# Later weights' maxima, scales and splits spread over layer 1: an interleaved attention and gMLP kernel

## The chip, the cores and the metric

The kernel runs on one core of a Trainium2 chip. The time is the device time of one execution in microseconds (us). A core has five engines that run at once, each with its own instruction queue: TensorE (PE; its weight loads are listed as PEld), VectorE (DVE), ScalarE (ACT), GpSimd (POOL) and SyncE (SP), which here issues all DMA transfers. Engines wait for each other by semaphores, and each one takes its instructions strictly in order: what waits holds up all that is queued behind it. TensorE multiplies from SBUF into PSUM; its clock can be halved for stretches, and the profile lists the granted clock.

## The reference

```python
def _A_ref(x, wq, wk, wv, wo, beta):          # 2048 x 640, 32 heads of 20, 4 segments of 512
    q, k, v = heads of x @ wq, x @ wk, x @ wv
    for s in range(N):
        logits = jnp.einsum("bhqd,bhkd->bhqk", qs, ks) * scale + mask
        a_dot = jnp.einsum("bhqk,bhkd->bhqd", _softmax(logits), vs)
        pq = phi(qs)
        a_mem = einsum(pq, M) / (einsum(pq, z)[..., None] + 1e-6)
        outs.append(g * a_mem + (1.0 - g) * a_dot)
        M = M + einsum("bhld,bhle->bhde", phi(ks), vs);  z = z + phi(ks).sum(l)
    return o @ wo

def _B_ref(x, w_in, w_sp, b_sp, w_out):
    z = _gelu(x @ w_in)                        # w_in 640 x 1728
    z1, z2 = z[..., :Fh], _layernorm(z[..., Fh:])
    g = w_sp @ z2 + b_sp[:, None]              # w_sp 2048 x 2048
    return (z1 * g) @ w_out                    # w_out 864 x 640

x = x + _A_ref(_layernorm(x), ...);  x = x + _B_ref(_layernorm(x), ...)
x = x + _A_ref(_layernorm(x), ...);  x = x + _B_ref(_layernorm(x), ...)
```

The two layers use the same weights.

## The kernel before

Every large product is made of three fp16 matmuls: each operand is split into a high and a low half (h and l), and h·h, h·l and l·h are summed. A weight therefore goes through a chain once, in layer 1: its absolute **maximum** over the whole matrix is found (tile by tile on VectorE, L192, from tiles named wmst into a table wap); a power of two becomes its **scale** (`pow2_max` and `pow2_spread`: the column of maxima is turned with TensorE, wtp, reduced, put on a diagonal, wdg, and spread to all partitions by a second matmul, wbc); and each tile is loaded again (wst) and **split**: the high half by ScalarE (L84), the low half by VectorE (L85). The split weight is then kept in HBM (`keep`, w_oh and so on), and layer 2 only loads it.

There are seven weights. q, k and v are made in the head of the program. The other four are the subject here: o (the attention's output, 640x640), i0 and i1 (the halves of w_in, each 640x864; i1 makes z2 and i0 makes z1) and u (w_out, 864x640).

Layer 1 runs in this order: head; attention over 64 pairs of heads; the mixer's first half (`phase1b`: norm, w_in, gelu, z2's norm, in tiles of 128 tokens, and the attention's output product for four of them); its second half (`phase2`: w_sp, gate, w_out). Layer 2 is the same with another form of the w_sp product (`phase2s`).

In attention a step t is a third of a pair. Each pair has scores computed twice: mp with queries in rows, of which VectorE takes the row maximum mx (L1304), and es with keys in rows, which ScalarE turns to P by exp (L1297). The maxima go through TensorE's transpose mtp (one for each pair) and ScalarE and VectorE's mr into two rows of the tile qk by DMA, so that es comes out with the maximum taken off. ScalarE casts P to PH, GpSimd takes the difference PL (L1315; VectorE does some in the last four pairs), and pv is the product of PH and PL with the values. Between them run the dense products: vps, qps, kps (values, queries, keys), yps (output).

The order on TensorE is written out by hand (`run`: streams of jobs, each with its step t). On the other engines a scheduler orders the instructions from the order of the program text, priorities (`high_priority`) and its own estimate of when things are ready. The stream `background` in `run` placed the work on the four weights: all 32 maxima at 0.75 steps apart from step -8, the scales at steps 50 to 53, o's splits from step 55, i1's from step 69. The tiles for these loads (tag bg, two buffers) are shared with the o tiles of the output product. i0 was loaded and split at the head of `phase1b`, at high priority but into memory that attention's last work still used, with stage tiles of 864 columns.

In `phase1b`, xn is the normed tile, xnhl its two halves, th their transpose, which enters w_in; zp is the product.

Of the kernel before, what the change touches and what calls it, by code (L numbers as in the profile page):

```python
# [46 lines left out]
WNAMES = ["v", "q", "k", "o", "i0", "i1", "u"]  # L47
# [18 lines left out]
def pow2_spread(g, psum, tag, dg, c0, n):  # L66
# [3 lines left out]
    nc.tensor.matmul(bc[:, :n], g.ones8[:n, :], dg[:n, :n], start=True, stop=True)  # L70
    pw = g.pw[:, c0:c0 + n]
    nc.vector.tensor_copy(pw, bc[:, :n])
# [15 lines left out]
class Weight:  # L88
# [17 lines left out]
    def load(self, stage, width=864, tag="wst", keep=True):  # L106
# [4 lines left out]
        if self.made:  # L111
# [5 lines left out]
            return  # L117
        for k in range(self.nk):
# [23 lines left out]
def attn_weights(g, ctx, wv, wq, wk, wo, w_in, w_out):  # L142
# [6 lines left out]
    g.wi = [Weight(g, "i0", 4, w_in, 0, FH), Weight(g, "i1", 5, w_in, FH, FH)]  # L149
# [4 lines left out]
    g.esc, g.rq, g.rk, g.gq, g.gk, g.sig, g.epsd, g.yw, g.zi, g.pofs = s(0), s(1), s(2), s(3), s(4), s(5), s(6), s(7), (s(8), s(9)), s(10)  # L154
# [24 lines left out]
def other_scales(g, a, pool, psum, tag):  # L179

    nc = g.nc
    last = None
    for i, w in enumerate((g.wo, *g.wi, g.wu)):
        width = D if w.cols == D else w.cols // 2
        j = 0
        for k in range(w.nk):
            n = min(128, w.dram.shape[0] - 128 * k)
            for c in range(0, w.cols, width):
                t = a.bg.tile([128, D], F32, tag="bg", name="wmst")[:n, :width]
                nc.sync.dma_start(t, w.dram[k * 128:k * 128 + n, w.c0 + c:w.c0 + c + width])  # L190
                if last is not None:
                    nc.vector.tensor_reduce(*last, AX.X, ALU.max, apply_absolute_value=True)  # L192
                last = g.wap[:n, i, j:j + 1], t
                yield True
                j += 1
    nc.vector.tensor_reduce(*last, AX.X, ALU.max, apply_absolute_value=True)
    yield 50
# [1407 lines left out]
```

## Time and profile before

| | us |
|---|---|
| median of 3 runs | 2320.95 (2319.37 to 2323.72) |
| profiled execution | 2323.64 |
| its span, first to last instruction | 2321.4 |
| layer 1's attention, mtp of the first pair to that of the last | 99.5 to 624.0 |
| layer 1's mixer, first half | 646.7 to 848.6 |
| layer 2's attention, first mtp to last | 1274.8 to 1764.4 |
| layer 2's mixer, first half | 1787.0 to 1979.5 |

A window row gives the busy time of each engine in a stretch, and the share of full clock that TensorE was granted. A group row gives shape, count, busy time, mean duration of one in ns, the idle time of the engine just before, and what ended it. A wait row says who waited for whom: total, times, longest.

### The profile page before, as it was taken

What the parts mean: (1) busy time and instruction counts of PE and PEld (TensorE: products, weight loads), DVE (VectorE), ACT (ScalarE), POOL (GpSimd) and SP (SyncE); (2) the same over time, 40 slices, a digit from 0 to 9 for tenths busy, and PEclk for the clock granted to TensorE, in tenths of its full rate; (3) what the DMA queues carried; (4) which work ended last, traced back from release to release, by engine and by line L of the source; (5) the groups of instructions that cost most, each with busy time, mean ns of one, the idle gap of its engine ahead of it and who ended that gap; (6) DMA issues with size and microseconds to landing.
All of it is one profiled execution on the core that took longest, in us unless ns stands there. A gap on an engine that the chain in (4) does not pass through costs nothing.

```text
span 2321.4 us, 50384 instructions
## 1 busy us (share of the span) xinstructions
PE 2172.0 (94%) x20490; PEld 1298.3 (56%) x20490; DVE 1498.8 (65%) x2792; ACT 1174.5 (51%) x1452; POOL 971.0 (42%) x726
## 2 busy tenths in 40 slices
PE   4878799899989999999999988999998999999999
PEld 2445465556645555556554555656665555555655
DVE  7678868887744545445434788787776767546545
ACT  3379678788732232122212797887875424322321
POOL 2178688888710000000001688888885323000000
PEclk9999899999999999999999999999999999999999
DMA  5654544644662458778555336453467434877875
GB/s 162 165 140 101 128 113 126 131 137 124 149 178 84 134 161 212 230 194 236 165 139 157 75 92 182 107 123 93 121 168 168 113 93 110 252 208 199 211 215 136
DMA packets 509704, 350.14 MB, mean 151 GB/s; under 512 B 409312, under 2 KB 444768, under 8 KB 504352
## 3 DMA queue, kind: packets, MB, share of 16 engines
q1 hardware_dynamic: 509472, 346.93, 56.7%
q8 instruction: 160, 2.62, 0.5%
q14 instruction: 72, 0.59, 0.1%
HBM read 160.83 MB, written 97.93 MB: 111 GB/s over the span
## 4 chain that ended last, share of the span: by engine, by line
PE 65%; DVE 10%; DMA 7%; ACT 7%; issue 3%; POOL 2%; SPq 1%; ACTq 0%; DVEq 0%; POOLq 0%
PE zp L316 14%; PE gp L683 12%; PE cyp L715 3%; PE yps L1098 3%; PE cyp L518 3%; PE pv L1341 3%; DVE mx L1304 3%; PE ga L469 3%; PE kps L1122 3%; ACT P L1297 3%; PE mp L1288 2%; PE qps L1122 2%; PE gb L469 2%; PE vps L1065 2%; ACT PH L1314 2%
## 5 line engine op out<-in xcount | busy, mean ns | idle before, releaser
L1315 POOL TENSOR_TENSOR PL<-P,PH 128x1280 f16<-128x1280 f32 x248 | 649.7, 2622 | 167.2 <-ACT PH L1314 156.9
L1304 DVE TENSOR_REDUCE mx<-mp 128x2 f32<-128x1024 f32 (+3 forms) x512 | 408.8, 818 | 99.6 <-PE mp L1260 98.0
L1297 ACT ACTIVATE P<-es,sc 128x1024 f32<-128x1024 f32 (+1 forms) x384 | 370.3, 964 | 133.9 <-PE es L1260 131.3
L1314 ACT CAST PH<-P 128x1280 f16<-128x1280 f32 x256 | 320.4, 1253 | 22.0 <-PE pv L1341 14.1
L219 POOL TENSOR_TENSOR lnrs<-lnve,mhalf 128x1 f32<-128x1 f32 x92 | 56.0, 618 | 572.4 <-DVE lnve L218 572.4
L316 PEld LDWEIGHTS <-th 128*128 128x128 f16 x1920 | 188.2, 98 | 174.2 <-issue 13.0
L683 PE MATMUL gp<-zh,wt 128*128 128x432 f16 x1024 | 231.4, 346 | 0.2 <-DMA wt<-wn 0.2
L683 PEld LDWEIGHTS <-wt 128*128 128x128 f16 x1536 | 150.2, 98 | 129.4 <-DMA wt<-wn 0.6
L1288 PEld LDWEIGHTS <-qk 60*128 60x128 f16 (+1 forms) x2048 | 91.5, 94 | 226.0 <-issue 154.8
L469 PEld LDWEIGHTS <-wt 128*128 128x128 f16 x1344 | 131.5, 98 | 112.6
L1288 PE MATMUL mp<-qk 60*128 60x512 f16 (+3 forms) x1024 | 138.3, 307 | 42.1 <-DVE mx L1304 41.1
L1341 PE MATMUL pv<-vs,PH 128*128 128x41 f16 x2560 | 168.7, 183 | 1.7 <-DVE ab L1357 1.7
L1260 PEld LDWEIGHTS <-big 64*128 64x128 f16 x3072 | 141.8, 96 | 50.8 <-issue 4.2
L1341 PE MATMUL pv<-vs,PL 128*128 128x41 f16 x2560 | 164.6, 182 | 4.1 <-POOL PL L1315 3.6
L1288 PE MATMUL es<-qk 64*128 64x512 f16 (+3 forms) x1024 | 135.6, 300 | 34.1 <-ACT P L1297 25.4
L1065 PE MATMUL vps<-wvh,xt 128*128 128x320 f16 x640 | 152.5, 304 | 4.8 <-DVE vs L1071 4.1
L1341 PEld LDWEIGHTS <-PH 128*128 128x128 f16 x2560 | 143.1, 96 | 18.5
L316 PE MATMUL zp<-wi1h,th 128*128 128x432 f16 x640 | 148.2, 346 | 2.0 <-DVE x L1104 1.3
L1341 PEld LDWEIGHTS <-PL 128*128 128x128 f16 x2560 | 143.6, 97 | 7.2 <-POOL PL L1315 4.5
L683 PE MATMUL gp<-zl,wt 128*128 128x432 f16 x512 | 135.3, 346 | 0.0
L1122 PE MATMUL kps<-xt,wkh 128*128 128x512 f16 x380 | 122.6, 390 | 9.3 <-DVE phl L1156 9.2
L696 DVE TENSOR_TENSOR u<-u,cz 128x864 f32<-128x864 f32 x16 | 17.0, 1060 | 160.8 <-ACT u L694 114.6
(257 smaller groups left out, 4383.5 us busy)
## 6 DMA issues: line engine op xcount, KB each, us to landing
wr<-in_B_w_sp_dram SPq DMA_DIRECT2D x32, 1024.0 KB
qk<-st SPq DMA_DIRECT2D x256, 120.0 KB
x<-x SPq DMA_DIRECT2D x56, 320.0 KB
z<-z SPq DMA_DIRECT2D x32, 432.0 KB
cz<-z SPq DMA_DIRECT2D x32, 432.0 KB
turned<-wt SPq DMA_DIRECT2D x24, 512.0 KB
wt<-turned SPq DMA_DIRECT2D x24, 512.0 KB
st<-qhl SPq DMA_DIRECT2D x40, 256.0 KB
```

The lines of the kernel that those rows point to most:

```text
L316: nc.tensor.matmul(zp[:, n, :FHH], a[:, k, :], b[:, k, c:c + FHH], start=(k == 0 and j == 0), stop=(k == KD - 1 and j == 2))
L469: nc.tensor.matmul(o[:, :FHH], wt[:, x, m, :], zb[b][:, y, m, :], start=start and i == j == 0, stop=i == NP - 1 and j == 2, skip_group_che ...
L683: nc.tensor.matmul(gp[:, n, :FHH], ready[t][:, k % 2, a, k // 2, :], b[:, k, n * FHH:(n + 1) * FHH], start=(i == 0 and j == 0), stop=(i == ...
L1065: nc.tensor.matmul(ps, a[:, k, c], b[:, k, n * 320:(n + 1) * 320], start=(i == 0), stop=(i == 14))
L1122: nc.tensor.matmul(ps, a[:, k, c], b[:, k, :], start=(i == 0), stop=(i == 14))
L1260: nc.tensor.matmul(out, g.big[r, 64 - 64 * s:192 - 64 * s], mk, start=False, stop=s == 1, skip_group_check=True)
L1288: nc.tensor.matmul(out[:, h, o:o + w], a[r, ac], b[r, bc], start=o == 0, stop=False, skip_group_check=True)
L1297: self.last_of["ACT"] = nc.scalar.activation(P[:, :, 512 * c:512 * c + ew], es[:, :, :ew], AF.Exp, scale=g.esc).ins
L1304: self.last_of["DVE"] = nc.vector.tensor_reduce(self.mx[m][:, :, i], mp[:, :, o:o + w], AX.X, ALU.max).ins
L1314: nc.scalar.copy(PH, P[:, h])
L1315: (nc.gpsimd if h == 0 or n < self.N - self.TAIL else nc.vector).tensor_tensor(PL, P[:, h], PH, ALU.subtract)
L1341: nc.tensor.matmul(pv[:, i, h, :], x[:, c:c + 128], v[:, j, h0 + h, :], start=(j == 0 and x is PH), stop=(j == i and x is PL), skip_group_ ...
```

## The change

It touches five things.

1. **Maxima.** `other_scales` now takes a list of weights, a first step and a pace. o and i1 (15 tiles) are done from step -8 on, 1.9 steps apart; i0 (10 tiles) from step 121, 3 apart; u (7 tiles) in the mixer's first half, a piece after each of its tiles. The tiles have a pool of their own with three buffers, and a tile's maximum is taken two loads later instead of one.
2. **Scales.** The maxima over partitions no longer go through TensorE: the column is stored to a small HBM tensor (wmax), read back by a DMA that gives all of it to every partition (wmall), and reduced on VectorE. This is done three times: o with i1, i0, u. The scale's arithmetic (`pow2_floor`) is the same.
3. **Splits.** A stream of their own, `weights`: o from step 50 at 1.6 steps, i1 from step 124 at 2.4, with a pool of three buffers; each split is issued after the load of the next tile (ahead=1). i0 goes in tiles of 432 columns at the end of layer 1's attention, with a lower priority than before, behind the instructions that the first mixer tile's loads stand behind.
4. **Memory.** The pools of `phase1b` are laid out so that i0's tiles no longer lie on memory that attention's last pairs use; the norm's output goes into the tile it reads or into the x tile; one stage tile of `phase2` moves to the other side. The weights i0 and i1 are kept from within the mixer's loop.
5. The cast and store of an attention output tile (`out` in `combine`) stand one step later, but for the last pair.

```diff
-WNAMES = ["v", "q", "k", "o", "i0", "i1", "u"]
+WNAMES = ["v", "q", "k", "o", "i1", "i0", "u"]
...
-    def load(self, stage, width=864, tag="wst", keep=True):
+    def load(self, stage, width=864, tag="wst", keep=True, ahead=0):
...
-                st = stage.tile([128, 864 if tag == "wst" else D], F32, tag=tag, name="wst")[:n, :w]
+                st = stage.tile([128, {"wst": FH, "w0": FHH}.get(tag, D)], F32, tag=tag, name="wst")[:n, :w]
                 nc.sync.dma_start(st, self.dram[k * 128:k * 128 + n, self.c0 + c:self.c0 + c + w])
+                todo.append((self.h[:n, k, c:c + w], self.l[:n, k, c:c + w], st, self.c))
                 yield
-                split_scaled(self.g, self.h[:n, k, c:c + w], self.l[:n, k, c:c + w], st, self.c)
-                yield
+                if len(todo) > ahead:
+                    split_scaled(self.g, *todo.pop(0))
+                    yield
...
-def other_scales(g, a, pool, psum, tag):
+def other_scales(g, pool, ws, c0, at, pace):
...
-                t = a.bg.tile([128, D], F32, tag="bg", name="wmst")[:n, :width]
+                t = pool.tile([128, D], F32, tag="wm", name="wmst")[:n, :width]
                 nc.sync.dma_start(t, w.dram[k * 128:k * 128 + n, w.c0 + c:w.c0 + c + width])
-                if last is not None:
-                    nc.vector.tensor_reduce(*last, AX.X, ALU.max, apply_absolute_value=True)
-                last = g.wap[:n, i, j:j + 1], t
-                yield True
+                last.append((g.wap[:n, i, j:j + 1], t))
+                if len(last) > 2:
+                    nc.vector.tensor_reduce(*last.pop(0), AX.X, ALU.max, apply_absolute_value=True)
+                yield at
+                at += pace
...
-    nc.vector.tensor_reduce(g.wam[:, 3:7], g.wap, AX.X, ALU.max)
-    yield 51
-    dg = pow2_max(g, pool, psum, tag, g.wam, 3, 4)
-    yield 53
-    pow2_spread(g, psum, tag, dg, 3, 4)
...
+    nc.vector.tensor_reduce(g.wam[:, c0:c0 + n], g.wap[:, c0 - 3:c0 - 3 + n], AX.X, ALU.max)
+    yield at + 3
+    t = pool.tile([128, D], F32, tag="wm", name="wmall")[:, :128 * n]
+    d = nc.dram_tensor(f"wmax{c0}", (128, n), F32, kind="Internal").ap()
+    nc.sync.dma_start(d, g.wam[:, c0:c0 + n])
+    yield at + 6
+    nc.sync.dma_start(t, d.rearrange("(o p) n -> o (p n)", o=1).to_broadcast((128, 128 * n)))
+    yield at + 11
+    nc.vector.tensor_reduce(g.pw[:, c0:c0 + n], t.rearrange("q (p n) -> q n p", n=n), AX.X, ALU.max)
+    pow2_floor(g, c0, n)
...
-        with tc.high_priority(offset=HP if w0 is None else 2 * HP):
-            for _ in g.wi[0].load(sp):
-                pass
...
-            xn = pe1.tile([128, D], F32, tag="xn", name="xn")
+            xn = x1 if t < NWO else xt
...
+        with tc.high_priority(offset=2 * HP) if w0 is not None else first():
+            for _ in g.wi[0].load(sp, FHH, "w0", False, 1):
+                pass
+        more = () if g.wu.made else other_scales(g, wm, (g.wu,), 6, 0, 0)
...
+            if w0 is None and i in (3, 6):
+                g.wi[i == 3].keep()
+            if i > 2:
+                next(iter(more), None)
...
-        self.post(2, out)
+        self.post(2 if n + 1 == self.N else 3, out)
...
+                yield from other_scales(g, self.wm, (g.wo, g.wi[1]), 3, -8, 1.9)
...
+                yield 120
+                yield from other_scales(g, self.wm, (g.wi[0],), 5, 121, 3)
...
+        def weights():
...
+            yield 49
+            for w, width, at, pace in (g.wo, D, 50, 1.6), (g.wi[1], FHH, 124, 2.4):
+                w.tiles(g.top[w is not g.wo])
+                for i, _ in enumerate(w.load(self.ws, width, "ws", w is g.wo, 1)):
+                    yield at + pace * i
```

What stands where on the engines can be read from the two programs. TensorE's order is the same but for two instructions that go, wtp and wbc of the four scales.

On VectorE, around the scales (rs and ab belong to the pair's output, qhl, qps, kps and phl to queries and keys), stood before:

```order
L1357 TENSOR_TENSOR ab<-pv,rs 128x328
L1325 SCALAR_TENSOR_TENSOR mr<-mtp,mr 8x128
L60 TENSOR_REDUCE wmx<-wtp 4x1
L62 TENSOR_SCALAR wdg<-ident,wmx 4x4
L1139 SCALAR_TENSOR_TENSOR qhl<-qps,qhl 128x512
L1144 TENSOR_SCALAR qps<-qps,sc 128x512
L1304 TENSOR_REDUCE mx<-mp 128x2 x2
```

and now, for o and i1, between pairs 11 and 12 instead of 18 and 19:

```order
L1382 TENSOR_TENSOR ab<-pv,rs 128x328
L1329 TENSOR_REDUCE mx<-mp 128x2 x2
L222 TENSOR_REDUCE pw<-wmall 128x2
L1350 SCALAR_TENSOR_TENSOR mr<-mtp,mr 8x128
L1181 SCALAR_TENSOR_TENSOR phl<-kps,sc,phl 128x512
L79 TENSOR_SCALAR pw<-pw 128x2
L1329 TENSOR_REDUCE mx<-mp 128x2
```

The round through TensorE has become one reduction of the tile that came back by DMA.

On ScalarE, at the end of layer 1's attention and the first mixer tiles (z, zh, xnhl), stood before:

```order
L1314 CAST PH<-P 128x1280 x2
L1368 CAST ohl<-oat 128x640
L84 ACTIVATE wi0h<-wst,iv 128x864 x2
L322 ACT_TABLE_LOAD
L322 ACTIVATE z_11256<-zp_11225,sc 128x864
L84 ACTIVATE wi0h<-wst,iv 128x864 x2
L355 CAST zh<-z_11256 128x864
L231 CAST xnhl<-xn 128x640
L84 ACTIVATE wi0h<-wst,iv 128x864
L329 ACTIVATE z_11308<-zp_11277,sc 128x864
```

and now, from the last pair on (five of the ten splits stand above this piece):

```order
L1339 CAST PH<-P 128x1280
L90 ACTIVATE wi0h<-wst,iv 128x432
L1322 ACTIVATE P<-es,sc 128x2x512
L90 ACTIVATE wi0h<-wst,iv 128x432
L250 CAST xnhl<-x_11180 128x640
L1322 ACTIVATE P<-es,sc 128x2x256
L1339 CAST PH<-P 128x1280 x2
L90 ACTIVATE wi0h<-wst,iv 128x432 x3
L1393 CAST ohl<-oat 128x640
L340 ACT_TABLE_LOAD
L340 ACTIVATE z_11268<-zp_11237,sc 128x864
L347 ACTIVATE z_11320<-zp_11289,sc 128x864
```

All ten splits of i0 have moved ahead of the first z, between the casts of the last pair.

SP's queue at the same place (x and xt are tiles of the output product, th a transpose for the mixer, qk<-mr the maxima for the last pair's scores) held before:

```order
L1106 DMA x_0_8<-x_10535 128x640
L1089 DMA xt<-in_A_x_dram 128x640
L1327 DMA qk_220<-mr 2x4x128 x2
L1080 DMA_TRANSPOSE o<-o_2 128x10x128
L275 DMA x_11270<-x_0_2 128x640
L233 DMA_TRANSPOSE th<-xnhl 128x10x128
```

and now:

```order
L130 DMA wst<-in_B_w_in_dram 128x432
L1131 DMA x_0_8<-x_10522 128x640
L1114 DMA xt<-in_A_x_dram 128x640
L130 DMA wst<-in_B_w_in_dram 128x432
L1352 DMA qk_220<-mr 2x4x128 x2
L1105 DMA_TRANSPOSE o<-o_2 128x10x128
L130 DMA wst<-in_B_w_in_dram 128x432 x2
L252 DMA_TRANSPOSE th<-xnhl 128x10x128
```

The loads of i0 now stand between these transfers; the stage has two buffers, so each load beyond the second waits for a split of VectorE's.

More of the change, by code (lines that the diff above doesn't have):

```diff
@@ L70, in pow2_spread, with pow2_floor @@
     nc.tensor.matmul(bc[:, :n], g.ones8[:n, :], dg[:n, :n], start=True, stop=True)
+    nc.vector.tensor_copy(g.pw[:, c0:c0 + n], bc[:, :n])
+    return pow2_floor(g, c0, n)
+def pow2_floor(g, c0, n):
+    nc = g.nc
     pw = g.pw[:, c0:c0 + n]
-    nc.vector.tensor_copy(pw, bc[:, :n])
     nc.vector.tensor_scalar(pw.bitcast(I32), pw.bitcast(I32), 0x7F800000, None, ALU.bitwise_and)
@@ L117, in load @@
             return
+        todo = []
         for k in range(self.nk):
@@ L148, in attn_weights @@
     g.wo = Weight(g, "o", 3, wo, 0, D)
-    g.wi = [Weight(g, "i0", 4, w_in, 0, FH), Weight(g, "i1", 5, w_in, FH, FH)]
+    g.wi = [Weight(g, "i0", 5, w_in, 0, FH), Weight(g, "i1", 4, w_in, FH, FH)]
     g.wu = Weight(g, "u", 6, w_out, 0, D)
@@ L176, in attn_scalars @@
     nc.vector.tensor_scalar(g.epsd, g.epsd, g.sig, 1e-6, ALU.mult, ALU.mult)
-def other_scales(g, a, pool, psum, tag):
+def other_scales(g, pool, ws, c0, at, pace):
     nc = g.nc
-    last = None
-    for i, w in enumerate((g.wo, *g.wi, g.wu)):
+    last = []
+    for i, w in enumerate(ws):
+        i += c0 - 3
         width = D if w.cols == D else w.cols // 2
@@ L334, in phase1b @@
         ts = [*range(NWO - 4), *range(NWO, NT), *range(NWO - 4, NWO)]
-        with first:
+        with first():
             a = load(ts[0])
@@ L1478, in run @@
         g = self.g
+        first = not g.wo.made
+        self.wm, self.ws = [self.pool(n, 3) for n in ("awm", "aws")] if first else [None, None]
         g.top = [self.top.enter_context(g.tc.tile_pool(name=n, bufs=1, side="right", reuse_waits="tile")) for n in ("topi", "topo")][::-1]
-        streams = [[next(it), i, it] for i, it in enumerate((fills(), background(), dense(), reads()))]
+        streams = [[next(it), i, it] for i, it in zip((0, 1, 1.5, 2, 3), (fills(), background(), weights(), dense(), reads()))]
         def until(t):
@@ L1496, in run @@
             if t == 3 * N - 9:
-                self.first, self.end_of = self.ended(), [*self.last_of.values()]
+                self.first, self.end_of = self.ended, [*self.last_of.values()]
             f, c = divmod(t + self.LF, 3)
```

40 lines of the change are left out of this document (20 added, 20 removed).

## The prediction, made before the result was known

> **What bounds the kernel now.** First the engine line of the page: TensorE is busy for 94% of the span, so only its waits, and its time at a reduced clock, can be won.
>
> ```profile
> PE 2172.0 (94%) x20490; PEld 1298.3 (56%) x20490; DVE 1498.8 (65%) x2792; ACT 1174.5 (51%) x1452; POOL 971.0 (42%) x726
> ```
>
> Then the stretches. Layer 2 runs the same matmuls as layer 1 and makes no weights, so it shows what layer 1 would cost without that work. I marked both layers by the transpose mtp, one for each pair of heads: 64 in a layer, numbered from 0.
>
> ```profile
> L1322 PE MATMUL mtp<-ident,mx x64: 269/269/385, 99.5 to 624.0; 128*8 128x128 f32 x64
> L1322 PEld LDWEIGHTS mtp<-ident,mx x64: 83/83/95, 1274.8 to 1764.4; 128*8 128x8 f32 x64
> ```
>
> That is 524.5 us against 489.6. The windows below go from mtp 0 to 8, 16, 28, 44 and 63, then to the mixer's first zp and to its first gp; layer 1 stands above, layer 2 below. The columns are the window, its length, the busy time of PE, PEld, DVE, ACT and POOL, the granted TensorE clock, the DMA share and GB/s.
>
> ```profile
> 99.40:170.00 70.60, 55.74 (x749) 34.99 (x744) 54.66 (x104) 43.12 (x57) 36.75 (x21) 0.93 0.55 146
> 170.00:225.20 55.20, 49.23 (x752) 28.69 (x749) 44.88 (x86) 49.99 (x64) 49.56 (x29) 1.00 0.39 96
> 225.20:342.60 117.40, 100.09 (x1304) 65.45 (x1301) 89.16 (x179) 84.62 (x111) 87.94 (x62) 0.91 0.48 120
> 342.60:481.10 138.50, 126.05 (x1746) 80.08 (x1742) 115.69 (x225) 111.59 (x147) 115.33 (x83) 0.99 0.52 126
> 481.10:624.00 142.90, 137.29 (x1992) 88.73 (x1989) 106.73 (x215) 111.87 (x134) 121.62 (x82) 0.99 0.51 135
> 624.00:646.70 22.70, 20.61 (x250) 13.53 (x248) 15.93 (x26) 13.21 (x15) 15.71 (x14) 0.90 0.68 146
> 646.70:848.60 201.90, 194.51 (x1080) 106.12 (x1080) 101.42 (x204) 62.88 (x70) 19.24 (x31) 0.98 0.47 132
> ...
> 1274.80:1333.00 58.20, 52.42 (x750) 33.66 (x745) 41.88 (x79) 42.48 (x56) 36.51 (x21) 1.00 0.30 75
> 1333.00:1388.10 55.10, 49.21 (x752) 28.70 (x749) 44.88 (x86) 49.97 (x64) 49.50 (x29) 1.00 0.36 97
> 1388.10:1486.50 98.40, 90.87 (x1301) 59.52 (x1298) 80.64 (x162) 79.51 (x104) 86.82 (x62) 1.00 0.53 144
> 1486.50:1619.50 133.00, 125.79 (x1742) 80.15 (x1738) 109.08 (x217) 107.71 (x139) 114.00 (x83) 0.99 0.45 111
> 1619.50:1764.40 144.90, 137.53 (x1996) 88.80 (x1992) 106.60 (x215) 111.94 (x134) 121.77 (x82) 0.99 0.54 140
> 1764.40:1787.00 22.60, 20.44 (x250) 13.45 (x247) 15.96 (x26) 14.12 (x16) 15.64 (x14) 0.91 0.75 147
> 1787.00:1979.50 192.50, 191.70 (x1081) 105.61 (x1081) 130.35 (x227) 71.55 (x104) 59.45 (x62) 1.00 0.45 119
> ```
>
> With equal matmul counts, layer 1 takes longer by 12.4, 0.1, 19.0, 5.5, -2.0, 0.1 and 9.4 us. Call them stages 1 to 5, the tail, and the mixer's first half. The excess stands where the weights' work is: the 32 maxima in stage 1, the common scale and the wo splits in stage 3, the i1 splits in stage 4, the i0 splits in the mixer. The last stages are bound by TensorE (137.3 of 142.9 us busy); the early ones by VectorE and ScalarE around it.
>
> **The change part by part.** The prices, from the groups and waits of this trace (shape and count, then busy us and mean ns of one, then the idle time before and its releaser; in the wait rows total, times and longest):
>
> ```profile
> L192 DVE TENSOR_REDUCE wap<-wmst 128x1 f32<-128x432 f32 (+1 forms) x24 | 15.5, 649 | 10.2 <-DMA wmst<-in_B_w_in_dram 7.3 <-DMA wmst<-in_B_w_out_dram 2.7
> L85 DVE SCALAR_TENSOR_TENSOR wi1l<-wst,iv,wi1h x10: 652/763/2211, 314.0 to 465.3; 128x432 f16<-128x432 f32 x10
> L85 DVE SCALAR_TENSOR_TENSOR wi0l<-wst,iv,wi0h 128x864 f16<-128x864 f32 x5 | 5.6, 1117 | 7.8 <-ACT wi0h L84 7.8
> L84 ACT ACTIVATE woh<-wst,iv 128x640 f16<-128x640 f32 x5 | 4.1, 825 | 5.1 <-DMA wst<-in_A_wo_dram 5.1
> L84 ACT ACTIVATE wi1h<-wst,iv 128x432 f16<-128x432 f32 x10 | 6.5, 650 | 4.0 <-DMA wst<-in_B_w_in_dram 4.0
> PE wtp L58 <- DVE mr L1325: 2.3, 1, 2.3
> PE kps L1122 <- DVE phl L1156: 5.3, 1, 5.3
> PE zp L316 <- ACT wi0h L84: 5.9, 2, 5.3
> PE zp L316 <- DVE wi0l L85: 1.5, 3, 0.6
> L76 DVE RECIPROCAL iv<-pw 128x4 f32<-128x4 f32 x1 | 0.2, 178 | 0.0
> SPq L190 <- DVE wap L192: 6.9, 9, 2.4
> SPq L1327 <- ACT mr L1324: 104.0, 37, 9.6
> ```
>
> *Before pair 0.* By the order of instructions 2 maxima stand there instead of 7. One of those removed stood just ahead of the phl for which TensorE waited 5.3 us:
>
> ```profile
> 85.69 0.81 DVE L192 TENSOR_REDUCE wap<-wmst 128x1 f32<-128x640 f32 x1
> 86.42 0.74 DVE L1156 SCALAR_TENSOR_TENSOR phl<-kps,sc,phl 128x512 f16<-128x512 f32 x1
> ```
>
> I take its 0.8, so -1, with ends 0 and -3 (all five at 0.65).
>
> *Stage 1.* 25 maxima (24 and the last) become 13: the rest go to stage 5 (i0) and the mixer (u). Each of the 25 carried 12.4 / 25 = 0.50 us of excess, so 12 fewer give -6.0, and all 25 would give -12.4. In the row above VectorE also stands still for 10.2 us on loads that have not landed; three buffers instead of two and a pace of 1.9 steps instead of 0.75 end most of that, and the 6.9 us in which SP's queue was held by a full buffer. I take -8.
>
> *Stage 2.* It gets the common maximum of o and i1, a store of it, a broadcast load, one maximum over 128x2x128 and five tiny operations. At 0.18 us for a tiny one and a third of a us for each maximum this is some 1.6 us of VectorE, which has 44.9 of 55.2 us to do and no excess. Nothing waits for the result before the wo splits some 40 us later. The load waits on SP for the store to land; behind it queue the mr rows that the scores need. I take +0.5, with ends 0 and +2.4 (one wait like SP's longest above).
>
> *Stage 3.* Gone are the transpose and spread on TensorE with its wait of 2.3, the 2.4 us wdg (row further down), 2 of 7 splits, and the 5.1 us that ScalarE stood at a head of its queue waiting for a wo load, with the P activations queued behind it: the next load is now issued ahead of each split. Left are five wo splits. In stage 4, 8 i1 splits stand with 5.5 us of excess, 0.69 each; by ScalarE's 825 against 650 ns a wo split is 0.87, five 4.4, and I leave 1.1 for the rest: 19.0 - 5.5 gives -13.5. Ends: -17 (splits nearly hidden) and -7 (only the transpose's wait 2.3, as much again behind wdg's 2.4, and the two splits 1.4, rounded up).
>
> *Stage 4.* Eight splits become one, and two maxima: 1.5 us remains, -4, ends -3 and -5.5.
>
> *Stage 5.* This pays: 9 i1 splits, 8 maxima and the second scale come in. At the early stages' prices that is 9 x 0.69 + 8 x 0.50 = 10.2. Their cover is TensorE, with DVE at 106.7 of 142.9 us and ACT at 111.9; where the cover is complete the price is 0. I take +4, nearer to hidden because TensorE is the bound here. If the cover goes, what is late is the maximum mx, for which the next mp matmul waits.
>
> *Tail.* The ten i0 splits now stand between the last P and PL of attention. They add 6.5 us to ScalarE's 13.2, and 10 x 0.56 (half a wi0l row) to 10 x 0.76 (the wi1l median) to VectorE's 15.9, in 22.7 us. One mr comes after a split and two norm operations. Each load beyond the second waits on SP for a split, with mr, o and th transfers behind it. But w_i0 is needed 7 us after the tail, so not all of it must fit: +3, ends 0 and +6.
>
> *Mixer.* The 7.4 us of TensorE's waits on wi0 end, and the clock of 0.98 with them; layer 2's 192.5 us is the bound, -9.4. Seven maxima of u and 2.2 MB of kept i0 stay early in the mixer under a TensorE that is busy throughout; I leave 1 us: -8.4, ends -4 and -9.4. The norm in place, the moved pools and the later o splits: 0, with 2 us either way, since layer 2's order is the same but for a few rows.
>
> Eleven DMAs more (five i0 loads, three stores, three broadcasts) cost SP issue time alone; SP has it, since it waits for ScalarE's mr for 104.0 us of layer 1.
>
> Sum: -1 - 8 + 0.5 - 13.5 - 4 + 4 + 3 - 8.4 = -27.4. The profiled execution took 2323.64 us (span 2321.4 and 2.2 around it), so 2296.2; against the median of the runs, 2.7 us lower, 2293.5, which I predict. All good ends give 2272, all bad ones 2322.
>
> [...] The wdg is a 4x4 operation that took 2.40 us and ended with a POOL operation that started just before it:
>
> ```profile
> 241.51 2.40 DVE L62 TENSOR_SCALAR wdg<-ident,wmx 4x4 f32<-4x4 f32 x1
> 241.27 2.62 POOL L1315 TENSOR_TENSOR PL<-P,PH 128x1280 f16<-128x1280 f32 x1
> ```
>
> [...]
>
> **Rivals.** *The clock stays low (13%).* The halved clock may not come from the waits that go. Two stretches of stage 3:
>
> ```profile
> 236.00:246.30 10.30, 5.82 (x87) 2.99 (x81) 8.12 (x14) 6.48 (x8) 7.05 (x4) 1.00 0.54 130
> 246.30:256.60 10.30, 9.94 (x88) 7.29 (x89) 6.50 (x21) 3.35 (x4) 3.18 (x2) 0.50 0.08 24
> ```
>
> TensorE is busy 5.8 of 10.3 us and then at 0.50 for as long. If this came with the work on the pairs themselves, 0.07 x 70.6 + 0.09 x 117.4 + 0.02 x 201.9 = 19.6 us would stay: gain 8, 2313. For it: stage 1 is 79% busy in any case. Against: layer 2 stands at 1.00 in the same stages with the same pair work. [...]
>
> *VectorE becomes the bound late (slower, 10%).* If the items in stage 5 and the tail (9 + 8 + 10 and a scale, 28) cost what stage 3's ten (7 splits, 3 for the scale) did, 1.9 us, they cost 53 against the 34.4 won elsewhere (1 + 8 - 0.5 + 13.5 + 4 + 8.4): 2340. It decides from 1.23 us an item. For: in stage 5 VectorE would reach 106.7 + 9 x 0.76 + 8 x 0.65 + 1.6 = 120 of 142.9 us. Against: TensorE bounds there, and the loads are no longer late.
>
> *It evens out (5%).* Every term at its bad end, or the low clock with stage 5 and the tail at their upper ends: 2322.
>
> **How the numbers follow.** The forecast (2274 to 2306) has 70%, still more gain 2%. The range takes in the low-clock case and leaves out the slower one: 2276 to 2316. Within 0.2% (4.6 us, about what a measurement of this kernel can tell) 5%; slower 10%; faster the rest, 85%.
>
> **What would show it.** Right: mtp 0 to 63 in layer 1 takes some 504 us, stage 3 near 104 at a clock over 0.95, no wtp after the head, the mixer's first half near 193, and zp waiting for no wi0. Wrong: stage 5 over 150 us with mp waiting for mx; the tail over 27; stage 3 still at 0.91.

## The result, and the profile after

The changed kernel takes 2318.81 us (median of 20 runs), the kernel before 2320.98 (20 runs): a ratio of 0.9987, with a 95% interval of 0.9977 to 0.9997. That is 2 us faster, or 0.1%. The prediction was 2293.5, so 25 of the 27 us that it expected are missing. The profiled execution has a span of 2318.9 us, against 2321.4, so the two traces can be compared stage by stage.

The engine line of the page of the changed kernel hardly differs from the one before:

```profile
PE 2172.1 (94%) x20487; PEld 1298.4 (56%) x20487; DVE 1507.4 (65%) x2807; ACT 1174.7 (51%) x1457; POOL 972.0 (42%) x726
```

The transpose mtp, once for each pair of heads, marks layer 1 and layer 2:

```profile
L1347 PE MATMUL mtp<-ident,mx x64: 269/270/385, 96.3 to 617.9; 128*8 128x128 f32 x64
L1347 PE MATMUL mtp<-ident,mx x64: 269/270/385, 1272.6 to 1763.0; 128*8 128x128 f32 x64
```

Layer 1's attention takes 521.6 us where 504 was forecast (before: 524.5). The windows of layer 1 in the changed kernel, with the columns and cuts of the prediction (window, length, busy time of PE, PEld, DVE, ACT and POOL, granted clock, DMA share, GB/s):

```profile
96.20:160.20 64.00, 55.14 (x747) 34.78 (x742) 48.54 (x92) 42.55 (x56) 36.49 (x20) 0.95 0.45 107
160.20:215.60 55.40, 49.31 (x750) 28.82 (x747) 46.15 (x93) 49.92 (x64) 49.52 (x29) 1.00 0.42 97
215.60:321.60 106.00, 95.47 (x1303) 61.97 (x1299) 86.03 (x167) 83.19 (x109) 88.36 (x62) 0.95 0.49 131
321.60:453.90 132.30, 125.75 (x1746) 79.90 (x1743) 111.46 (x220) 108.25 (x140) 114.17 (x83) 0.99 0.47 118
453.90:617.90 164.00, 143.13 (x1995) 91.29 (x1991) 123.67 (x240) 119.61 (x147) 124.19 (x82) 0.95 0.61 147
617.90:643.60 25.70, 21.51 (x245) 14.06 (x246) 21.10 (x37) 15.61 (x20) 15.89 (x13) 0.88 0.81 223
643.60:847.10 203.50, 194.33 (x1080) 105.99 (x1080) 103.25 (x214) 58.84 (x66) 18.75 (x31) 0.98 0.49 131
```

Beside the terms of the prediction, with the lengths taken from one execution each:

| | before | after | forecast | measured |
|---|---|---|---|---|
| head, to the first mtp | 99.5 | 96.3 | -1 | -3.2 |
| stage 1 | 70.6 | 64.0 | -8 | -6.6 |
| stage 2 | 55.2 | 55.4 | +0.5 | +0.2 |
| stage 3 | 117.4 | 106.0 | -13.5 | -11.4 |
| stage 4 | 138.5 | 132.3 | -4 | -6.2 |
| stage 5 | 142.9 | 164.0 | +4 | +21.1 |
| tail | 22.7 | 25.7 | +3 | +3.0 |
| mixer, first half | 201.9 | 203.5 | -8.4 | +1.6 |

The five early terms came in near their sum: together -27.2 against -26. Of that, 21.1 us are given back in stage 5 and 3.0 in the tail, and the mixer loses 1.6 where it should have gained 8.4. (Layer 2's stage 3, which the change leaves alone, reads 98.4 in one trace and 102.6 in the other; a stage of one execution is not to be read closer than that.)

What TensorE waited for in stage 5, before and then after (total, times, longest):

```profile
PE mp L1288 <- DVE mx L1304: 3.3, 4, 2.3
PE es L1288 <- DMA qk<-mr: 2.3, 2, 2.1
```

```profile
PE es L1313 <- DMA qk<-mr: 11.7, 6, 4.6
PE mp L1313 <- DVE mx L1329: 5.8, 6, 2.6
PE mtp L1347 <- DVE rs L1377: 1.2, 1, 1.2
```

TensorE's waits rose by 13.1 us in all; most of the rest is its clock, 0.95 in this stage instead of 0.99. The larger wait is not for VectorE. It is for the small transfer that carries the maxima of a pair (2 KB) into the rows of qk. The longest of these waits, in TensorE's timeline and SP's queue just ahead of it (start, length, instruction):

```profile
570.29 0.61 PE L1313 MATMUL es<-qk 64*128 64x512 f16 x2 [4.59 <-DMA qk<-mr]
```

```profile
559.43 0.35 SPq L148 DMA_DIRECT2D w_i1h<-wi1h  x1
559.87 0.38 SPq L148 DMA_DIRECT2D w_i1l<-wi1l  x1
560.30 2.39 SPq L1397 DMA_DIRECT2D o<-ohl  x2
562.74 2.52 SPq L1352 DMA_DIRECT2D qk<-mr  x2
```

The first two are the store of the split i1: 2.2 MB in two transfers. The program text has it in the mixer's loop, but it stood in SP's queue as soon as its splits were done. In the mixer the waits of TensorE and VectorE now read:

```profile
PE zp L334 <- DMA th<-xnhl: 9.1, 3, 5.1
```

```profile
DVE wap L206 <- DMA wmst<-in_B_w_out_dram: 12.6, 3, 9.0
DVE pw L222 <- DMA wmall<-wmax: 8.5, 1, 8.5
```

The 7.4 us of waits for wi0 are gone, as forecast, and 9.1 us for th stand in their place; the clock of the stretch, which was to rise with the end of the waits, is 0.98 as before. VectorE stood still for u's loads and for the read-back of u's scale, and what the next tile needs was queued behind. Two of TensorE's three waits, and VectorE ahead of the second of them:

```profile
670.82 0.90 PE L334 MATMUL zp<-wi1h,th 128*128 128x432 f16 x2 [5.05 <-DMA th<-xnhl]
686.99 0.54 PE L334 MATMUL zp<-wi1h,th 128*128 128x432 f16 x2 [2.79 <-DMA th<-xnhl]
```

```profile
682.52 0.29 DVE L222 TENSOR_REDUCE pw<-wmall 128x1 f32<-128x128 f32 x1 [8.46 <-DMA wmall<-wmax]
682.72 0.81 DVE L251 TENSOR_TENSOR xnhl<-x,xnhl 128x640 f16<-128x640 f32 x1
```

The last row makes the low half of which th is the transpose; it ends at 683.5, and zp starts 3.5 us later.

### The profile page after: what moved, and what is told of

The parts are those of the page before. It is cut to its first block, busy times and chain, and to the rows that moved or that the text cites. A ratio compares the mean times of both kernels' runs of the same rounds, so it can differ in the third digit from the quotient of the medians.

```text
span 2318.9 us, 50405 instructions
## 1 busy us (share of the span) xinstructions
PE 2172.1 (94%) x20487; PEld 1298.4 (56%) x20487; DVE 1507.4 (65%) x2807; ACT 1174.7 (51%) x1457; POOL 972.0 (42%) x726
## 4 chain that ended last, share of the span: by engine, by line
PE 60%; DVE 4%; ACT 4%; DMA 3%; issue 2%; POOL 1%; SPq 0%; ACTq 0%; DVEq 0%; POOLq 0%
PE zp L334 13%; PE gp L709 12%; PE cyp L741 4%; PE cyp L544 3%; PE ga L495 3%; PE gb L495 3%; PE pv L1366 2%; PE vps L1090 2%; PE yps L1123 2%; PE qps L1147 2%; PE mp L1313 2%; PE ge L495 2%; PE gd L495 2%; PE gc L495 2%; PE kps L1147 1%
## 5 line engine op out<-in xcount | busy, mean ns | idle before, releaser
L495 PEld LDWEIGHTS <-wt 128*128 128x128 f16 x1344 | 131.4, 98 | 112.7 <-DMA wt<-wn 0.2
L1366 PEld LDWEIGHTS <-PH 128*128 128x128 f16 x2560 | 142.9, 96 | 18.6 <-issue 0.2
```

The source lines that it names most:

```text
L495: nc.tensor.matmul(o[:, :FHH], wt[:, x, m, :], zb[b][:, y, m, :], start=start and i == j == 0, stop=i == NP - 1 and j == 2, skip_group_che ...
L1366: nc.tensor.matmul(pv[:, i, h, :], x[:, c:c + 128], v[:, j, h0 + h, :], start=(j == 0 and x is PH), stop=(j == i and x is PL), skip_group_ ...
```

## The experiments

The theories: T, bulk transfers of weights (stores of split weights, loads) stand ahead of the small ones that TensorE waits for; W, the items themselves (splits, maxima, scales on VectorE and ScalarE) are what costs. After the first four runs a third was added: Q, an engine's queue stands still behind an instruction that waits for a late transfer. "Loses" is against the same pair of layer 2 in the same trace, from mtp to mtp. In the changed kernel stage 5 loses 3.2 us at pairs 45 to 49, 3.6 at 51 and 52, 3.0 at 53 and 54, 7.4 at 57 and 58 and 2.9 at 60 to 62: 20.1 in all, where the kernel before gains 1.9.

**The store in pieces.**

```diff
                     split_scaled(self.g, *todo.pop(0))
+                    self.store(done)
+                    done += 1
...
-            if w0 is None and i in (3, 6):
-                g.wi[i == 3].keep()
```

The new `store` sends, for i0 and i1 alone, the rows of a block as soon as all its columns are split.

> Against the changed kernel (2318.8): the split weights i1 and i0 go to HBM in five pieces each, a piece as soon as its rows are split, instead of 2.2 MB at once; 16 DMA issues more on SP, nothing else moves. Theory T (bulk transfers stand ahead of the small ones that TensorE waits for): the 4.6 us for which es waited for the maxima's rows right after the i1 store goes, with the half clock behind it, so pairs 57 and 58 of layer 1 lose at most 2 us against layer 2 instead of 7.4; in the mixer's first half half of the 9 us for which zp waited for th goes (199 instead of 203.5 us); sum -8 to -10, 2309 to 2311. Theory W (the splits and maxima on VectorE and ScalarE themselves are the cost): stage 5 stays at 164 us, the mixer at 203, and the issues cost 0 to 3 us: 2318 to 2322.

Measured: 2312.5 us, 0.9969 of the kernel before (0.9957 to 0.9980). The same two pairs, 57 and 58, in the changed kernel and then with the store in pieces:

```profile
559.90:580.60 20.70, 16.11 (x218) 10.13 (x215) 10.43 (x21) 10.77 (x13) 12.02 (x9) 0.84 0.71 202
```

```profile
561.40:575.10 13.70, 13.26 (x215) 8.88 (x212) 10.17 (x21) 10.61 (x13) 11.99 (x9) 1.00 0.56 159
```

VectorE, ScalarE and POOL do the same work in both. The loss falls from 7.4 to 0.5 us, wait and half clock together: T for this place. The other runs agree: in the five traces that have the whole i1 store at pair 57, the changed kernel's among them, pairs 57 and 58 lose 5.2 to 7.4 us, in the seven other variants of the changed kernel at most 0.5. The mixer did not gain (205.5 us), so T's second half failed; there the i0 store at once is not what holds th. The tail rose by 2.6 us.

**The same store in the kernel before.**

```diff
                     yield 55 + 14 * j + pace * i
+            if new:
+                yield 166
+                g.wi[1].keep()
```

> Against the kernel before (2321.0), which stores i1 at pair 43 at no cost: the same 2.2 MB are stored once more at pair 57, ahead of a transpose, two o stores and the rows of the maxima for the next pair, as in the changed kernel; no split, maximum or scale stands near. Theory T: pairs 57 to 59 lose 4 to 8 us against layer 2, TensorE waiting for qk by mr: 2325 to 2329. If the loss at these pairs of the changed kernel came from the work on VectorE and ScalarE ahead of them, the store costs nothing here either: 2321.

Measured: 2324.7, 1.0020 (1.0010 to 1.0031). Pairs 57 and 58 of the kernel before as it is, then with the second store, and what TensorE waited for there:

```profile
577.40:590.60 13.20, 13.20 (x216) 8.90 (x212) 10.20 (x20) 10.61 (x13) 11.68 (x8) 1.00 0.55 149
```

```profile
575.40:592.70 17.30, 14.67 (x213) 9.38 (x210) 10.13 (x20) 10.56 (x13) 11.65 (x8) 0.90 0.73 207
```

```profile
PE yps L1098 <- DMA o<-o: 2.6, 1, 2.6
```

(`new` is true in layer 1 alone.) 2.2 MB with no split near cost 4.1 us at these pairs. The transfer that comes late is another one (the transposed o, waited for 2.6 us, where the changed kernel waited 4.6 us for the rows of the maxima). At pair 43 the same store cost nothing; there SP issued the next rows of the maxima 8.3 us after it, in the changed kernel 3.3 us after it (562.74 against 559.43, above). That this distance decides is argued, not tried:

```profile
475.94 0.40 SPq L136 DMA_DIRECT2D w_i1h<-wi1h  x1
...
484.24 0.51 SPq L1327 DMA_DIRECT2D qk<-mr  x1
```

**Where the i1 splits stand.**

```diff
-            for w, width, at, pace in (g.wo, D, 50, 1.6), (g.wi[1], FHH, 124, 2.4):
+            for w, width, at, pace in (g.wo, D, 50, 1.6), (g.wi[1], FHH, 69, 2.4):
```

> Against the changed kernel: the ten splits of i1 stand from step 69 on, as in the kernel before, with their three buffers and a load ahead kept; the i1 store goes with them, from pair 57 to pair 39. Theory T: the store costs less at pair 39, as it cost nothing at pair 43 of the kernel before; stage 5 falls from 164 to about 154 (pairs 57 and 58 alone give 7.4, the i1 loads some more), stage 4 rises from 132.3 to 134; 2310 to 2313. Theory W: 9 of the 18 items leave stage 5 at 21 / 18 = 1.2 us each, -10.5, and come back in stage 4 at the 5.5 of the kernel before: 2314. If pairs 57 and 58 stay slow without the store, T falls.

Measured: 2315.5, 0.9976 (0.9966 to 0.9985). Stage 5 falls to 149.0, below both expectations, and stage 4 rises to 141.6, above both. Pairs 46 to 52 lose nothing any more, though the maxima of i0 still stand there; 57 and 58 lose nothing. In stage 4, 6.0 of the 9.4 us lost against layer 2 lie at pairs 37 and 38 (pair 39 gains 2.3). They are not the store's: it is issued at the end of pair 38, after a wait for P in pair 37 with a low clock behind it (0.79 and 0.77 in the two pairs), and TensorE waits for no transfer in the 12 us after it:

```profile
406.53 0.28 PE L1313 MATMUL es<-qk 64*128 64x256 f16 x2 [2.25 <-ACT P L1322]
```

```profile
421.35 0.49 SPq L148 DMA_DIRECT2D w_i1h<-wi1h  x1
```

So the store is free at a third place. The tail rose by 4.9, with TensorE waiting for P; the order on ScalarE changed there too.

**Where the maxima and the scale of i0 stand.**

```diff
-                yield 120
-                yield from other_scales(g, self.wm, (g.wi[0],), 5, 121, 3)
+                yield 72
+                yield from other_scales(g, self.wm, (g.wi[0],), 5, 73, 3)
```

> Against the changed kernel: the ten maxima of i0 and its scale stand from step 73 on instead of 121, so in the first half of stage 4 and not in stage 5. Theory W: 8 items of 18 leave stage 5 at 1.2 us each, -9, and cost 0 to 5 in stage 4: 2310 to 2315; pairs 46 to 49 lose nothing any more. Theory T: the waits for the maxima mx at pairs 46, 47 and 49 (3.5 us with what follows) go, and the wait at pair 54 behind the scale's broadcast (2.5), but the waits for the maxima's rows at pairs 57 and 58 stay at 7.4; -6 and 0 to +3 in stage 4: 2313 to 2316.

Measured: 2318.7, 0.9995 (0.9983 to 1.0008). Stage 5 falls by 8.5 to 155.5, stage 4 rises by 7.3. Both theories were wrong on pairs 46 to 49: they lose the same 3.2 us without any maximum there. With the kernel above this settles it: those 3.2 us are the i1 splits; the maxima beside them are free. Pairs 51 to 56, without the scale and the last of the maxima, lose nothing. The scale went on to cost at its new place, by a wait of TensorE that was not there before:

```profile
PE mp L1313 <- DVE iv L83: 3.8, 1, 3.8
```

VectorE's timeline at that place, and GpSimd's:

```profile
418.40 2.57 DVE L80 TENSOR_TENSOR pw<-pw,floor 128x1 f32<-128x1 f32 x1
...
421.38 2.17 DVE L1495 TENSOR_SCALAR sc<-pw 128x2 f32<-128x2 f32 x1
```

```profile
418.34 5.18 POOL L1340 TENSOR_TENSOR PL<-P,PH 128x1280 f16<-128x1280 f32 x2
```

Two operations of one or two elements a partition took 2.57 and 2.17 us, and end with the two PL; the other tiny ones took 0.15.

**Through TensorE instead.**

```diff
+    if psum is not None:
+        ...
+        dg = pow2_max(g, wx, psum, "ms", g.wam, c0, n)
+        yield at + 5
+        pow2_spread(g, psum, "ms", dg, c0, n)
+        return
...
-                yield from other_scales(g, self.wm, (g.wi[0],), 5, 121, 3)
+                yield from other_scales(g, self.wm, (g.wi[0],), 5, 121, 3, self.pl1, self.pm)
```

> Against the changed kernel: the scale of i0 alone goes through TensorE (transpose, maximum, diagonal, second matmul) as in the kernel before, at the same place in stage 5, instead of the store and the read-back. By the prices of the kernel before this costs 2.3 us of TensorE waiting and 2.4 of VectorE, so if the round trip by DMA were free the time would rise by 2 to 5: 2321 to 2324. If the round trip is what pairs 51 to 56 lose (6.6 us with the i1 splits there, 4.4 with the store in pieces, 0 without it), stage 5 falls by 2 to 4: 2315 to 2317. Equal within 2 us: the way of the scale does not matter.

Measured: 2319.9, 0.9989 (0.9977 to 1.0002); stage 5 is 162.4. The way of the scale does not matter for i0 in stage 5: the read-back by DMA costs as much there as the round through TensorE that it replaced.

**u out of the mixer.**

```diff
+                yield from other_scales(g, self.wm, (g.wu,), 6, 40, 3)
...
-        more = () if g.wu.made else other_scales(g, wm, (g.wu,), 6, 0, 0)
+        more = ()
```

> Against the changed kernel: the seven maxima of u and its scale stand from step 40 on in attention, none in the mixer; the loads of 2.2 MB that stood right behind the i0 store at the head of the mixer go with them. Theory T: of 4.4 MB ahead of the first transposes th half is gone; the waits of zp for th fall from 9.1 to 3 to 5 us and the mixer's first half from 203.5 to 198; in stages 2 and 3 the maxima cost 7 x 0.50 = 3.5 at the early stages' price: 2315 to 2318. Theory W: the mixer gains only what VectorE's seven maxima held up there, 0 to 1 us, and attention pays 3.5: 2321 to 2323.

Measured: 2327.5, 1.0022 (1.0011 to 1.0033), slower than either theory. The mixer fell to 195.3 us, more than forecast. But TensorE had two long waits, one in stage 3 (114.6 us) and one ahead of the mixer, in the tail (38.5 us):

```profile
PE es L1313 <- ACT P L1322: 7.8, 2, 7.1
...
PE zp L334 <- DMA th<-xnhl: 15.9, 1, 15.9
```

By a reading of the queues that no further run tried, in the first ScalarE's next cast, with P behind it, stood for a buffer whose o store had been issued right behind the store of wo (1.6 MB), and in the second the loads of the mixer's first tiles had come to stand behind the i0 store. The order around both had moved with u, so this run does not price u alone.

**Bulk work held back.**

```diff
-            z1_half(t, w_in_half(0, *th))
+            sent = z1_half(t, w_in_half(0, *th))
...
-            if w0 is None and i in (3, 6):
-                g.wi[i == 3].keep()
-            if i > 2:
-                next(iter(more), None)
+            if w0 is None:
+                with ExitStack() as held:
+                    for j in (*last, sent):
+                        held.enter_context(tc.issue_after(j))
+                    if i in (3, 6):
+                        g.wi[i == 3].keep()
+                    if i > 2:
+                        next(iter(more), None)
```

> Against the changed kernel (2318.8): the stores of i1 and i0, the loads of u for its maxima, its scale's store and read-back and the maxima themselves are each held behind the z1 store and the norm of a tile of the mixer's first half (i1 after tile 3, i0 after tile 6, u one piece a tile from tile 3); attention and the splits are unchanged. Theory Q (an engine's queue stands still behind an instruction that waits for a late transfer: VectorE for u's loads and the read-back of its scale, with the norms of the next tiles behind it): zp waits for th no more than 1.5 us in all, the mixer's first half falls from 203.5 to 193 to 196; with the i1 store gone from pair 57 stage 5 falls by 7 to 157. Sum -15, 2303 (2300 to 2307). Rival P (the splits of i0 in the tail and the new places of the mixer's tiles make the first tiles late): the mixer stays over 200, and only stage 5 gains: 2311.

Measured: 2318.6, 0.9988 (0.9977 to 0.9999). Stage 5 fell to 154.5, below the 157 expected, and the mixer's first half to 198.4, a little over; zp still waited 2.8 us for th. The sum failed: the mixer's second half, at 425.4 in the changed kernel, took 439.0, because TensorE's first products there waited:

```profile
PE gp L713 <- DMA wt<-wn: 11.1, 2, 8.9
```

**u faster.**

```diff
-                    if i > 2:
+                    for _ in range(2 if 0 < i < 4 else 1):
                         next(iter(more), None)
```

> Against the held kernel (2318.6): u goes at two loads a tile from the mixer's tile 0 on, so its scale is done after tile 8 instead of tile 13; the stores of i1 and i0 stay behind tiles 3 and 6. In the held kernel the mixer's first half fell by 5 us and the second half rose by 13.7: its first products gp waited 11 us for wt, the turned w_sp, whose row load wr came 25 us later than in the changed kernel. If that load waited for the memory of u's tiles, it comes early again: second half 425 instead of 439, first half 195 to 199, and the kernel comes to 2305 (2301 to 2309). If the 4.3 MB of stores moved into the mixer are the cause, the second half stays over 435 and the time at 2318.

Measured: 2307.9, 0.9953 (0.9939 to 0.9967): faster than both kernels. The mixer's two halves:

```profile
637.40:835.70 198.30, 191.86 (x1080) 105.34 (x1080) 103.07 (x213) 59.15 (x66) 19.82 (x31) 1.00 0.58 148
835.70:1261.00 425.30, 421.58 (x2502) 243.07 (x2501) 191.63 (x333) 93.34 (x106) 18.57 (x21) 1.00 0.71 192
```

The second half is back while both stores are still in the mixer, so u's tiles, held to tile 13, were the cause: the first load of w_sp's rows (wr) was issued at 810.8 us in the held kernel and at 774.0 here. That it is by their memory, which this load takes next, is argued and not shown. With u's loads spread, VectorE stands 1.1 us for them and not at all for the read-back, as theory Q has it, and the clock is 1.00. But zp still waits 4.3 us for th, and the first half stays 5 us over the 193 of the prediction; this rest was not tried.

**Held, and i0's maxima at step 29.** The edit is the held one, with i1's store in pieces and `(g.wi[0],), 5, 29, 2` in place of the stage 5 line.

> Against the changed kernel: as the held kernel, but the i1 store in five pieces in attention, and the ten maxima of i0 with its scale from step 29 on at 2 steps, right behind those of o and i1. Theory Q: stage 5 loses only what the i1 splits cost at pairs 46 to 51 (4.6) and the end of attention (3), 151 instead of 164; stage 2 and 3 pay 0 to 4 for the ten maxima and the scale, since loads that arrive in time cost little; mixer 194; 2298 (2294 to 2303). Theory W (a price for each maximum wherever it stands, 0.5 to 0.65, and 2.4 for the scale): stages 2 and 3 pay 8: 2302 to 2306.

Measured: 2318.0, 0.9982 (0.9968 to 0.9997), with the 13.6 us of the late second half in it. Stage 5 is 149.6, near the 151 expected; stages 2 and 3 pay 7.5 (169.0 against 161.5; 5.6 against the held kernel's 163.4), nearer to W's figure than to Q's. Ten maxima and a scale thus cost some 5.5 to 7.5 us in stages 2 and 3, as in stage 4; in stage 5 the maxima are covered and the scale is not.

**i0 back in the mixer.**

```diff
+        with tc.high_priority(offset=HP if w0 is None else 2 * HP):
+            for _ in g.wi[0].load(sp, FH, "wst", False):
+                pass
...
-            xn = x1 if t < NWO else xt
+            xn = pe1.tile([128, D], F32, tag="xn", name="xn")
...
```

The pools go back with it, and u's tiles share i0's stage tiles.

> Against the held kernel: i0 is loaded and split at the head of the mixer's first half at high priority in tiles of 864 columns, with the pools and the norm's own tile of the kernel before; all else as in the held kernel. If the move of the i0 splits into the tail is worth something, as the prediction had it (tail +3, mixer -8.4), this kernel is 3 to 7 us slower than the held one, with zp waiting 6 to 8 us for wi0 again: tail 22.7 and mixer 201. If the splits in the tail cost more than the waits that they end, it is as fast or faster: tail 22.7, pairs 60 to 63 without the 2 to 3 us that they lose in the changed kernel, mixer 199 to 202.

Measured: 2323.9, 1.0015 (1.0001 to 1.0029), 5.3 us slower than the held kernel. Stage 5 and tail, which have no i0 split, are 5.1 us shorter (149.4 and 25.1 for 154.5 and 25.1); the mixer's first half is 210.3 for 198.4. zp waits 6.6 us for wi0 again. The move of i0, with the pools that belong to it, is worth some 5 us.

**i1 early, with the store held.** The edit of i1 above, on the kernel with u faster.

> Against the kernel with u faster: the ten i1 splits from step 69 on, without their store in attention. In stage 5 the splits cost 3.2 us at pairs 46, 47 and 49 in every kernel that has them there, whether the maxima of i0 stand beside them or not, and some 1.5 later. If stage 5 hides less than stage 4, the time falls by 2 to 4; if the splits cost in stage 4 the 5.5 of the kernel before, it rises by 1 to 2. I expect stage 5 at 149 (from 154.5) and stage 4 at 135 to 137 (from 131.6): equal within 2 us.

Measured: 2311.6, 0.9971 (0.9954 to 0.9988), some 4 us slower, with intervals that overlap (five runs each). Stage 5 is 149.8 instead of 155.6, stage 4 138.0 instead of 131.4, and the tail again 29.9 for 26.0. What stage 5 gains stage 4 loses within a microsecond, less than such a stage differs between traces; the 4 us lie in the tail. Which of the two stages hides the splits better is not shown.

**No load ahead.**

```diff
-                for i, _ in enumerate(w.load(self.ws, width, "ws", w is g.wo, 1)):
+                for i, _ in enumerate(w.load(self.ws, width, "ws", w is g.wo, int(w is not g.wo))):
```

> Against the changed kernel: each of the five wo splits is issued before the load of the next tile instead of behind it, as in the kernel before; three buffers and the steps stay, and i1 keeps its load ahead. By the prediction's third stage ScalarE then stands again up to 5.1 us for wo loads with the P activations behind it: stage 3 from 106.0 to 109 to 111, 2322 to 2324. If three buffers and a wider pace alone did it: stage 3 at 106 to 107, no change.

Measured: 2321.1, 1.0004 (0.9995 to 1.0014). Stage 3 rises from 106.0 to 109.8 (105.8 to 108.2 in the nine traces that leave this stage alone), and ScalarE's waits in it have the wo loads again:

```profile
ACT woh L90 <- DMA wst<-in_A_wo_dram: 7.6, 4, 3.2
```

The load ahead is worth some 3 us of the 11.4 won in stage 3.

## Why the prediction was wrong, and where it was right

- **Head to stage 4** (forecast -26, measured -27.2): right, and nearer in the sum than in the terms: the head and stage 4 gained 2.2 us more each, beyond their best ends, and stages 1 and 3 gained 1.4 and 2.1 less. Of stage 3, the load ahead is shown by an experiment; the rest (no transpose, two splits fewer, wider pace) is argued from the same rows as before the run. The rival that the clock stays low was half right for these stages: stage 3 stands at 0.95 instead of 0.91, just at the mark that the prediction set, and stage 1 at 0.95 instead of 0.93. Reckoned as the prediction does, 8.5 us of the 15.5 lost to the clock in the two stages remain (0.05 x 64.0 + 0.05 x 106.0).
- **Stage 5** (+4, measured +21.1): wrong. The term held nine splits, eight maxima and a scale, and asked only whether TensorE covers them on VectorE. The runs show the i1 splits at 3.2, the scale at some 3, the maxima at 0, and 7.4 for the i1 store, which the term did not contain at all. That missing store is the step that failed here. The prediction named the store of i0 for the mixer, at 1 us with the maxima of u, and none for i1, although the store had moved to pair 57 with the splits. "Wrong: stage 5 over 150 us with mp waiting for mx" came true in its number; the wait was for transfers, twice as much as for mx. The rival that VectorE becomes the bound had the right place and, for its largest part, the wrong mechanism. The 2.9 at pairs 60 to 62 are the first i0 splits: with i0 back in the mixer these pairs lose nothing in sum. Most of it is one split, which ran beside a PL of GpSimd and took 2.73 us, where the shortest took 0.65; TensorE's next transpose waited behind it:

```profile
614.09 2.73 DVE L91 SCALAR_TENSOR_TENSOR wi0l<-wst,iv,wi0h 128x432 f16<-128x432 f32 x1
```

```profile
613.74 2.61 POOL L1340 TENSOR_TENSOR PL<-P,PH 128x1280 f16<-128x1280 f32 x1 [0.84 <-ACT PH L1339]
```

```profile
617.93 0.38 PE L1347 MATMUL mtp<-ident,mx 128*8 128x128 f32 x1 [2.11 <-DVE lnve L237]
```

  The 3.6 us at pairs 51 and 52 are in this trace a wait of 1.94 us for the rows of the maxima, once more a transfer, and the clock of 0.57 behind it (last section). With the splits and the scale both in place they were 0.2 to 2.1 us in the other kernels, and nothing where either had moved; what makes that transfer late stays open.
- **Tail** (+3, measured +3.0): right in size by luck, not in its reason. With i0 back in the mixer the tail is 25.1 us all the same, though by other waits (2.4 us for x and 2.1 for PL); what the i0 splits cost lies a little earlier, at pairs 60 to 62. What the tail's 2.4 to 3 us come from was not tried. The ten low halves have a median of 0.87 us, and the one of 2.73 is the only one that held TensorE up.
- **Mixer** (-8.4, measured +1.6): the waits for wi0 went as forecast, and by the run with i0 put back their move is worth its price. The step that failed here is "seven maxima of u and 2.2 MB of kept i0 stay early in the mixer under a TensorE that is busy throughout; I leave 1 us". Of the mixer's 203.5 us TensorE was busy for 194.3, but VectorE was not free: it stood 12.6 us for u's loads and 8.5 for the read-back, with the norm of the next tile behind it, and th came late. Held back and spread, the same work left 198.3 us.
- **The rest** (0): measured -1.0, right in the changed kernel. It is not safe ground: 13.6 us were lost there when u's tiles were held too long.

The largest part of what stage 5 lost and the mixer's loss are thus of one kind: a slow transfer in front of something that has to be quick, once in SP's queue and once in VectorE's.

## What to carry to other kernels

When a change moves work, list the transfers that go with it, stores too, in their size, and look what the same queue issues right behind them: 2.2 MB were free where the next urgent transfer came 8.3 us later, and cost 7 us where it came 3.3 us later, with no change in any engine's work. A store that nobody waits for should go in pieces (here 0.5 us lost at two pairs instead of 7.4), or behind an instruction that marks a quiet place; here program order alone did not hold it. An instruction that waits for a round trip must not stand in an engine's queue ahead of the next tile's work (VectorE stood 8.5 us for u's read-back), and buffers held longer for that reason have to be checked against whoever takes their memory next (13.6 us here, the memory as the cause argued and not shown).

## What was not expected of the hardware

Two tiny operations of VectorE, `pw<-pw,floor` and `sc<-pw`, took 0.11 and 0.15 us in stage 5 of the changed kernel, where GpSimd had no PL from 544.32 to 546.76, and 2.57 and 2.17 us beside PL, above. There they end at 420.97 and 423.55; the two PL end at 423.52 together, and half of their 5.18 us is over at 420.93. Not all that runs beside PL is held: `iv<-pw`, between the two, took 0.15 us at 421.31. What tells them apart, no run here shows. So a chain of tiny operations is not always cheap where GpSimd is busy: here two of them took 4.74 us.

A low clock did not need a long wait here. After a single wait of 1.94 us in the changed kernel (TensorE's timeline, then two windows) the next 4 us stood at 0.57:

```profile
516.91 0.39 PE L1313 MATMUL es<-qk 64*128 64x512 f16 x2 [1.94 <-DMA qk<-mr]
```

```profile
514.00:518.00 4.00, 2.06 (x42) 1.21 (x38) 3.27 (x6) 2.58 (x4) 2.58 (x2) 1.00 0.97 318
518.00:522.00 4.00, 4.00 (x24) 1.58 (x23) 2.34 (x6) 2.88 (x4) 2.96 (x2) 0.57 0.00 1
```

The stretch ahead was busy for 2.06 of 4 us. Behind the 4.59 us wait of pair 57 the clock was lower, 0.50 from 571 to 575 us. How long a wait has to be for the clock to fall, no run here shows.

A round trip by DMA took 12.0 us, part of it with the DMA engines idle. In the changed kernel u's column of maxima (512 B) was issued at 670.51, and its read-back, which waits for it with nothing else issued after the z store at 670.93, at 677.80; VectorE had the result at 682.52. From 674 to 678 the DMA engines did next to nothing (SP's queue, then two windows, with the DMA share next to last). In stage 5 SP waited 1.3 us for the same kind of store, here 6.4; what makes the difference was not tried:

```profile
670.51 0.33 SPq L218 DMA_DIRECT2D wmax<-wam  x1
670.93 0.38 SPq L348 DMA_DIRECT2D z<-z  x1
677.80 0.32 SPq L220 DMA_DIRECT2D wmall<-wmax  x1
```

```profile
674.00:676.00 2.00, 2.00 (x8) 0.90 (x7) 0.06 (x1) 0.00 (x0) 0.00 (x0) 0.64 0.00 0
676.00:678.00 2.00, 2.00 (x12) 1.07 (x11) 0.00 (x0) 0.00 (x0) 0.00 (x0) 1.00 0.09 8
```
